# First chunk of a linear-attention and expert kernel: wide rows, one tile for all batches, work by head pairs, and a retuned planner

## The chip, the cores and the metric

The kernel runs on one core of a Trainium2 chip. The metric is device time in microseconds (us). "Before" and "after" are the two kernels of the change. Every run was timed beside runs of the kernel before on the same chip. Some executions are slower (for the kernel before 2.6 to 3.7 per cent longer); only fast runs are compared unless the text says otherwise.

Engine names in the profile: PE is TensorE (PEld its weight loads), DVE is VectorE, ACT is ScalarE, POOL is GpSimd, SP is SyncE. A "q" behind a name (SPq) is that engine's queue of instructions that issue transfers. L278 is line 278 of that kernel's source.

## The reference, cut to what matters

```
# q, k, v, f_logit: 4 batches x 8 heads x 768 tokens x 48
f = 1 / (1 + exp(-f_logit))
for t in range(768):                       # recurrent state of 48x48 per batch and head
    state = f[t][:, None] * state + outer(k[t], v[t])
    y[t]  = q[t] @ state
x = y as 3072 x 384                        # tokens x (heads * 48)
p = probs / (sum(probs) + 1e-9)            # 3072 x 4
out = sum over e of p[:, e] * (relu(x @ w1[e]) @ w2[e])   # 4 experts, 384 -> 1024 -> 384
```

## The kernel before

The 768 tokens are cut into six chunks of 128. In a chunk the recurrence becomes matmuls: prefix sums of the log gates (`cs`), exponentials of them (`e`), products with Q and K (`qk`), transposes, masked scores (`AT`), outputs (`y`), and an update of the state (`kv`). Chunk c+1's attention is woven into the expert matmuls of chunk c. In chunks 0 and 1 TensorE transposes Q and K; from chunk 2 on a DMA does it.

Nothing waits dynamically for a free engine. A planner in the kernel simulates all operations at build time, with assumed costs, and emits them in that order. The order is then fixed for each engine, while semaphores make each instruction wait until its data is there:

```
class Plan:
    LATENCY = 0.2                          # assumed delay between engines
    ...                                    # (cut) list scheduling by priority, costs, free buffers

def add_load(c, nm, b, n, prio, deps=()):  # a load takes 1.05 us per batch of the DMA's time, lands 2.0 later
    op = P.add(f"ld {nm}{c}.{b}", {"DMA": 1.05 * n}, lambda e: load(c, nm, b, n), prio,
               deps=deps, takes=[(nm, c, b // 2)], lag=2.0)
...
et = P.add(f"tp {c}.{b}", {"DMA": 1.8}, on(dma_tp), s(4), deps=[qm, km], ..., lag=2.2)   # DMA transposes
```

The first chunk is loaded batch by batch, 128 tokens on 128 partitions, in rows of 48 floats (192 bytes):

```
nc.sync.dma_start(out=tl(nm, c, b // 2)[:, hh(b, n), :], in_=srcs[nm][c, :, b * H:(b + n) * H, :])
for i, x in enumerate("f0 k0 q0 f1 k1 q1 f2 f3 k2 q2 v0 k3 q3 v1 v2 v3".split()):
    add_load(0, x[0], int(x[1]), 1, -1000 + i)
```

Of the kernel before, what the change touches and what calls it, by code (L numbers as in the profile page):

```python
# [14 lines left out]
class Op:  # L15


    def __init__(self, name, costs, emit, prio, deps=(), takes=(), frees=(), lag=0.0):
        self.name, self.costs, self.emit, self.prio = name, costs, emit, prio
        self.deps = [d for d in deps if d is not None]  # L20
        self.takes, self.frees, self.lag = list(takes), list(frees), lag
        self.end = self.start = self.engine = None
        self.pad = 0


class Plan:


    LATENCY = 0.2

    def __init__(self, rooms):
        self.ops, self.rooms = [], {r: list(range(n)) for r, n in rooms.items()}
        self.slot, self.left = {}, {}

# [14 lines left out]
    def take(self, o):  # L49
        new = [k for k in o.takes if k not in self.slot]  # L50
        for r in {k[0] for k in new}:
            if len(self.rooms[r]) < sum(k[0] == r for k in new):
                return False
        for k in new:
            self.slot[k] = self.rooms[k[0]].pop(0)
        return True

    def run(self):
# [5 lines left out]
        free_at.update({"DMA": 0.8, "DVE": 5.0, "POOL": 3.5, "ACT": 2.1, "PE": 2.0})  # L64
        freeing, done, now = [], [], 0.0
        while left:
# [3 lines left out]
            for e in ("PE", "ACT", "DVE", "POOL", "DMA"):  # L70
                while free_at[e] <= now + 1e-9:
                    for o in left:
                        if e in o.costs:
                            t = self.ready(o, e)
                            if t is not None and t <= now + 1e-9 and self.take(o):
                                break
                    else:
                        break
                    left.remove(o)
                    o.engine, o.start, o.end = e, now, now + o.costs[e]  # L80
                    free_at[e] = o.end
                    for k in o.frees:
                        self.left[k] -= 1
                        if self.left[k] == 0:
                            freeing.append((o.end + self.LATENCY, k[0], self.slot[k]))
# [14 lines left out]
def kernel(  # L100
# [23 lines left out]
    NT = B * T  # L124
    ctx.enter_context(tc.manual_schedule())
# [8 lines left out]
    rooms = {"ps_m": 4, "ps_t": 4, "f": 4, "q": 4, "k": 4, "v": 4, "ex": 2, "gp": 4, "e": 3, "qk": 7,  # L134
             "vb": 7, "egs": 8, "QK": 2, "AT": 2, "yb": 2, "xT": 2, "h": 2, "o": 6}
    P = Plan(rooms)

# [22 lines left out]
    )  # L160
    Sf = const.tile([MP, B, NP, D], FP32)
# [15 lines left out]
    for nm, a in (("f", f_logit), ("q", q), ("k", k), ("v", v)):  # L177
# [4 lines left out]
        "f": ([T, 2 * H, D], FP32), "q": ([T, 2 * H, D], FP32), "k": ([T, 2 * H, D], FP32), "v": ([T, 2 * H, D], FP32),  # L182
# [4 lines left out]
        "KV": ([T, 512], FP32), "xp": ([T, KD, T], BF16), "hp": ([128, NT], FP32), "op": ([128, 512], FP32),  # L187
    }

    def tl(kind, *key):  # L190

        if (kind, key) not in tiles:
            room = kind if kind in rooms else "ps_m" if kind in ("hp", "op") else "ps_t"
            slot = P.slot[(room, kind) + key if room.startswith("ps_") else (room,) + key]
            if room in ("gp", "qk"):
# [25 lines left out]
    def load(c, nm, b, n):  # L221
        ins[c, nm, b] = nc.sync.dma_start(out=tl(nm, c, b // 2)[:, hh(b, n), :],  # L222
                                          in_=srcs[nm][c, :, b * H:(b + n) * H, :])
        if (c, nm, b) == (1, "f", 0):
            after(ins[c, nm, b], ins["w", 5])

    def load_w(i, e, which):
        w, r = (w1_sb, w1_r) if which == 1 else (w2_sb, w2_r)
        ins["w", i] = nc.gpsimd.dma_start(out=w[:, e], in_=r[e])
        if i == 0:  # L230
            after(ins["w", 0], ins[0, "k", B - 1])

    p_src = moe_domain_probs.rearrange("(b c p) e -> p b c e", p=128, c=C)
    p_dst = pt.rearrange("p (b c) e -> p b c e", c=C)

    def load_p(c):
        nc.sync.dma_start(out=p_dst[:, :, c], in_=p_src[:, :, c])
# [8 lines left out]
    def gate1(c, b, n):  # L246
        nc.scalar.activation(out=tl("ex", c, b)[:, 0:n * H], in_=tl("f", c, b // 2)[:, hh(b, n), :], func=AF.Exp, scale=-1.0)  # L247
# [4 lines left out]

    def pe_cs(c, b):
        g, cs = tl("gp", c, b // 2)[:, b % 2], tl("cs", c, b)
        nc.tensor.matmul(out=cs[:, 0:HD], lhsT=Ub, rhs=g[:, :, 0:D], start=True, stop=True)  # L255
        if c == 0:
            for i in range(NP):
                nc.tensor.matmul(out=cs[0:MP, HD + i:HD + i + 1], lhsT=flat(g, i)[:, 0:MP], rhs=ones, start=True, stop=True)

    def exps(c, b):  # L260
        cs, e = tl("cs", c, b), tl("e", c, b)
        nc.scalar.activation(out=e[:, 0].rearrange("t (d h) -> t h d", d=D), in_=cs[:, 0:HD].rearrange("t (i r d) -> t r i d", r=2, d=D),  # L262
                             func=AF.Exp, scale=-1.0)
        nc.scalar.activation(out=e[:, 1], in_=cs[:, 0:HD], func=AF.Exp)  # L264
        if c == 0:
            nc.scalar.activation(out=tl("egs", c, b), in_=cs[0:MP, HD:HD + NP], func=AF.Exp, scale=-1.0)
# [6 lines left out]
    def product(c, b, j, eng):  # L273
# [3 lines left out]
                                   in0=tl("qk"[j], c, b // 2)[:, hh(b), :].rearrange("t (i r) d -> t i r d", r=2),  # L277
                                   in1=e, op=ALU.mult)  # L278

    def cast_v(c, b, eng):  # L280
        copy(eng, tl("vb", c, b), tl("v", c, b // 2)[:, hh(b), :])
# [21 lines left out]
    def ev_at(c, b, r):  # L303
        nc.vector.tensor_tensor(out=tl("AT", c, b)[:, r].rearrange("s i t -> s (i t)"),  # L304
                                in0=tl("A", c, b, r).rearrange("s i t -> s (i t)"), in1=mask01, op=ALU.mult)

    def pe_y(c, b):
        y, AT, vb, QK = tl("y", c, b), tl("AT", c, b), tl("vb", c, b), tl("QK", c, b)
        for i in range(NP):
            if c > 0:  # L310
                nc.tensor.matmul(out=y[:, i * 2 * D:(i + 1) * 2 * D], lhsT=QK[0:MP, 0, i, :],  # L311
                                 rhs=Sb[c % 2][:, b, i, :], start=True, stop=False, skip_group_check=True)
            for r in range(2):
                h = 2 * i + r
                nc.tensor.matmul(out=y[:, h * D:(h + 1) * D], lhsT=AT[:, r, i, :], rhs=vb[:, h, :],  # L315
                                 start=(c == 0), stop=True, skip_group_check=True)
# [13 lines left out]
    def state(c, b):  # L330
        egs, nb = tl("egs", c, b), Sb[(c + 1) % 2]
# [37 lines left out]
    def store(c, nt, cols):  # L369
        r0 = nt * S + c * T  # L370
        nc.sync.dma_start(out=out[r0:r0 + T, cols], in_=tl("o", c, nt)[:, cols])
# [5 lines left out]
    def add_load(c, nm, b, n, prio, deps=()):  # L377
        op = P.add(f"ld {nm}{c}.{b}", {"DMA": 1.05 * n}, lambda e: load(c, nm, b, n), prio,
                   deps=deps, takes=[(nm, c, b // 2)], lag=2.0)
# [4 lines left out]
    for i, x in enumerate("f0 k0 q0 f1 k1 q1 f2 f3 k2 q2 v0 k3 q3 v1 v2 v3".split()):  # L384
        add_load(0, x[0], int(x[1]), 1, -1000 + i)
    wd = {}
    for i, (e, which) in enumerate(nw):
        iss = P.add(f"w issue {i}", {"POOL": 0.9}, lambda _, i=i, e=e, which=which: load_w(i, e, which),
                    -500 + i, deps=[ld[0, "k", B - 1]])
        wd[e, which] = wd[i] = P.add(f"w {i}", {"DMA": 4.5}, lambda _: None, -500 + (0, 1, 2, 3, 4, 5, 101.5, 103.5)[i], deps=[iss], lag=2.0)  # L390
    for half in range(2):
        for j, nm in enumerate("fkqv"):
            add_load(1, nm, 2 * half, 2, -400 + 4 * half + j, deps=[wd[5]])


    xdone, kvdone = {}, {}

    def attention(c, slot, gran):
        G, X, Y, GS = {}, [], [], []
        more = c < C - 1  # L400
        for b0 in range(0, B, gran):
            p, d, half = slot(b0, 0) - 0.5, 0.54 if gran == 1 else 0.84, b0 // 2
            g1 = P.add(f"gate1 {c}.{b0}", {"ACT": d}, lambda e, b0=b0: gate1(c, b0, gran), p,
                       deps=[ld[c, "f", b0]], takes=[("ex", c, b0)], frees=[("f", c, half)])
# [4 lines left out]
        for b in range(B):  # L409
# [5 lines left out]
            cs = P.add(f"cs {c}.{b}", {"PE": 0.17 if c else 0.36}, on(pe_cs), s(0),  # L415
                       deps=[G[b]], takes=[pt_("cs")], lag=0.2, frees=[("gp", c, half)])
            ex = P.add(f"exps {c}.{b}", {"ACT": 0.98 if c else 1.1}, on(exps), s(0) + 0.1, deps=[cs],
                       takes=[("e", c, b)] + ([("egs", c, b)] if c == 0 else []), frees=[pt_("cs")])
            GS.append(P.add(f"egs {c}.{b}", {"DMA": 1.0}, on(dma_egs), s(3), deps=[ex], takes=[("egs", c, b)],
                            frees=[("e", c, b)], lag=2.0) if c and more else None)  # L420
            pe = {"DVE": 0.6, "POOL": 1.0} if c < 2 else {"POOL": 1.0}
            qm = P.add(f"q {c}.{b}", pe, one(product, 0), s(4) - 0.2,
                       deps=[ex, ld[c, "q", b]], takes=[("qk", c, b)], frees=[("q", c, half), ("e", c, b)])
            km = P.add(f"k {c}.{b}", pe, one(product, 1), s(4) - 0.1,
                       deps=[ex, ld[c, "k", b]], takes=[("qk", c, b)], frees=[("k", c, half), ("e", c, b)])
            vb = P.add(f"v {c}.{b}", {"ACT": 0.52, "DVE": 0.36} if c == 0 else {"POOL": 0.5, "ACT": 0.52} if c == 1 else {"POOL": 0.5}, one(cast_v), s(4),
                       deps=[ld[c, "v", b]], takes=[("vb", c, b)], frees=[("v", c, half)])
            if c < 2:
                tq = P.add(f"tpq {c}.{b}", {"PE": 0.22}, on(pe_tp, 0), s(4), deps=[qm],
                           takes=[pt_("tp")], frees=[("qk", c, b)], lag=0.2)  # L430
                tk = P.add(f"tpk {c}.{b}", {"PE": 0.22}, on(pe_tp, 1), s(4) + 0.01, deps=[km],
                           takes=[pt_("tp")], frees=[("qk", c, b)], lag=0.2)
                et = P.add(f"ev_tp {c}.{b}", {"DVE": 0.69, "ACT": 1.05}, lambda e, b=b: copy(e, tl("QK", c, b)[0:MP], tl("tp", c, b)), s(4) + 0.1,
                           deps=[tq, tk], takes=[("QK", c, b)], frees=[pt_("tp")])
            else:
                et = P.add(f"tp {c}.{b}", {"DMA": 1.8}, on(dma_tp), s(4), deps=[qm, km], takes=[("QK", c, b)],
                           frees=[("qk", c, b)], lag=2.2)
            at = P.add(f"at {c}.{b}", {"PE": 0.35}, on(pe_at), s(7), deps=[et],
                       takes=[pt_("A", 0), pt_("A", 1)], lag=0.2, frees=[("QK", c, b)])
            eA = [P.add(f"ev_at{r} {c}.{b}", {"DVE": 0.7}, on(ev_at, r), s(7) + 0.1 + 0.1 * r, deps=[at],  # L440
                        takes=[("AT", c, b)], frees=[pt_("A", r)]) for r in range(2)]
            y = P.add(f"y {c}.{b}", {"PE": 0.4 if c else 0.28}, on(pe_y), s(11), deps=eA + [vb, kvdone.get((c - 1, b))],
                      takes=[pt_("y")], frees=[("QK", c, b), ("AT", c, b), ("vb", c, b)], lag=0.2)
# [4 lines left out]
            if c < 2:  # L448
                xt = P.add(f"xt {c}.{b}", {"PE": 0.17}, on(pe_xt), s(13), deps=[ey],
                           takes=[pt_("xp")], frees=[("yb", c, b)], lag=0.2)  # L450
# [3 lines left out]
            else:  # L454
                xdone[c, b] = P.add(f"xt {c}.{b}", {"DMA": 0.9}, on(dma_xt), s(13), deps=[ey], takes=[("xT", c)],
                                    frees=[("yb", c, b)], lag=2.2)
            X.append(xdone[c, b])
        for b in range(B if more else 0):
            on = lambda f, b=b: (lambda e: f(c, b))
            pt_ = lambda kind, b=b: ("ps_t", kind, c, b)  # L460
            s15 = slot(b, 15) if c else 2 + 2 * b
            kv = P.add(f"kv {c}.{b}", {"PE": 0.22}, on(pe_kv), s15, deps=[Y[b], X[B - 1] if c == 0 else None],
                       takes=[pt_("KV")], frees=[("vb", c, b), ("qk", c, b)], lag=0.2)
# [127 lines left out]
```

## Time and profile before

| | before |
|---|---|
| time | 305.1 us, median of the four runs (304.5 to 315.0, the last slow) |
| span of the profiled execution | 302.7 us, mean granted TensorE clock 0.999 |
| first expert matmul | 22.7 us |
| TensorE gaps over 0.3 us after 45 us | 1.0 us in all |

The second is the busy time in the stretch from 70 to 125 us, in which chunk 2's attention begins (columns: stretch, its length, then busy us and instructions of PE, PEld, DVE, ACT, POOL, granted clock, DMA share, GB/s):

```profile
70.00:125.00 55.00, 54.24 (x454) 34.76 (x460) 33.32 (x71) 33.08 (x62) 29.29 (x51) 1.00 0.85 163
```

### The profile page before, as it was taken

Reading aid. Unit: us, or ns where it says so; the run is one execution under the profiler, and the core shown is the slowest. Engines: PE = TensorE matmul, PEld = TensorE weight load, DVE = VectorE, ACT = ScalarE, POOL = GpSimd, SP = SyncE. Lnnn points to the kernel's source line nnn. Section 1 sums busy time; section 2 is a strip of 40 time slices with the busy share of each in tenths; the row PEclk is TensorE's granted clock in tenths of the full one; section 3 lists DMA queues with packets and bytes.
Section 4 is the critical chain, followed back from the end, with each engine's and each line's share of the span. In section 5 each row is a group of like instructions: output and inputs, shape, how many; then the busy total and the mean of one; then the engine's idle time right before and its main releaser. Section 6 shows DMA issues by size and latency. Waiting matters only on the chain.

```text
span 302.7 us, 5517 instructions
## 1 busy us (share of the span) xinstructions
PE 293.2 (97%) x2112; PEld 169.4 (56%) x2143; DVE 138.1 (46%) x273; ACT 170.8 (56%) x295; POOL 95.5 (32%) x157
## 2 busy tenths in 40 slices
PE   7899999999999999999999999999999999999995
PEld 5565555567775655455555555555555555555553
DVE  6774013787853764516555344544423443201223
ACT  5767654857865444676356475345566344475440
POOL 4584400409656237423426143522332100000000
PEclk9999999999999999999999999999999999999999
DMA  7999999954994589866997877301322201100003
GB/s 157 203 193 204 207 206 193 228 83 91 217 207 84 111 161 187 189 122 120 182 187 134 216 142 147 56 13 28 100 61 51 48 14 30 67 22 2 0 0 106
DMA packets 137355, 36.10 MB, mean 119 GB/s; under 512 B 128496, under 2 KB 135792, under 8 KB 137328
## 3 DMA queue, kind: packets, MB, share of 16 engines
q1 hardware_dynamic: 131568, 29.45, 49.1%
q0 software_dynamic: 5760, 6.29, 12.4%
q8 instruction: 17, 0.28, 0.4%
q14 instruction: 10, 0.08, 0.1%
HBM read 31.51 MB, written 4.72 MB: 120 GB/s over the span
## 4 chain that ended last, share of the span: by engine, by line
PE 88%; DMA 4%; DVE 2%; SPq 2%; issue 1%; POOL 1%; ACT 1%; DVEq 0%; ACTq 0%; POOLq 0%
PE ps_m L356 41%; PE ps_m L344 40%; DMA w_sb<-in_moe_w_dram 3%; PE ps_t L300 2%; SPq L222 2%; DMA f<-in_f_logit_dram 1%; PE ps_t L315 1%; PE ps_t L321 1%; PE ps_t L311 1%; PE ps_t L255 1%; PE ps_t L285 1%; DVE qk L276 1%; POOL qk L276 0%; DVE AT L304 0%; POOL Sf L335 0%
## 5 line engine op out<-in xcount | busy, mean ns | idle before, releaser
L352 ACT ACTIVATE h<-ps_m 128x512 bf16<-128x512 f32 (+1 forms) x171 | 98.3, 577 | 103.0 <-PE ps_m L344 92.9
L356 PE MATMUL ps_m<-w_sb,h 128*128 128x384 bf16 x776 | 153.0, 324 | 0.2
L344 PE MATMUL ps_m<-xT,w_sb 128*128 128x512 bf16 (+1 forms) x593 | 150.4, 362 | 2.1 <-DVE o L367 0.3
L356 PEld LDWEIGHTS <-h 128*128 128x128 bf16 x776 | 73.0, 98 | 57.0
L363 DVE SCALAR_TENSOR_TENSOR o<-ps_m,pn,o 128x384 f32<-128x384 f32 (+1 forms) x73 | 44.6, 611 | 96.8 <-PE ps_m L356 89.4
L344 PEld LDWEIGHTS <-w_sb 128*128 128x128 bf16 x624 | 59.8, 98 | 47.1 <-issue 0.7
L276 POOL TENSOR_TENSOR qk<-q,e 128x384 bf16<-128x384 f32 x19 | 22.8, 1204 | 64.9 <-ACT e L262 64.4
L304 DVE TENSOR_TENSOR AT<-ps_t,mask 128x512 bf16<-128x512 f32 x48 | 31.1, 683 | 19.2 <-PE ps_t L300 19.1
L335 POOL TENSOR_TENSOR Sf<-Sf,egs 48x192 f32<-48x192 f32 x40 | 20.4, 510 | 48.8 <-DVE Sf L328 46.8
L350 DVE TENSOR_SCALAR h<-ps_m 128x512 bf16<-128x512 f32 (+1 forms) x37 | 20.7, 572 | 22.0 <-PE ps_m L344 19.8
L276 POOL TENSOR_TENSOR qk<-k,e 128x384 bf16<-128x384 f32 x20 | 21.0, 1052 | 19.8 <-ACT e L264 12.9
L262 ACT ACTIVATE e<-ps_t 128x384 f32<-128x384 f32 x24 | 20.7, 864 | 3.7 <-PE ps_t L255 2.4
L328 DVE TENSOR_TENSOR Sf<-Sf,ps_t 48x192 f32<-48x192 f32 x40 | 14.0, 349 | 6.1 <-PE ps_t L321 5.3
L336 POOL CAST sb<-Sf 48x192 bf16<-48x192 f32 x40 | 13.6, 339 | 2.6
L365 ACT ACTIVATE o<-ps_m,pn 128x384 f32<-128x384 f32 x20 | 11.6, 580 | 3.9 <-PE ps_m L356 3.1
L264 ACT ACTIVATE e<-ps_t 128x384 f32<-128x384 f32 x24 | 13.0, 541 | 0.0
L556 PE MATMUL ps_m<-busy 128*128 128x256 bf16 x71 | 11.5, 301 | 1.3 <-DVE busy L140 1.3
L218 DVE CAST yb<-ps_t 128x384 bf16<-128x384 f32 x16 | 8.9, 555 | 7.4 <-PE ps_t L315 6.3
L247 ACT ACTIVATE ex<-f 128x768 f32<-128x768 f32 (+1 forms) x14 | 10.5, 748 | 3.1 <-DMA f<-in_f_logit_dram 2.9
L315 PE MATMUL ps_t<-vb,AT 128*128 128x48 bf16 x192 | 11.4, 184 | 0.7 <-DVE vb L218 0.7
L315 PEld LDWEIGHTS <-AT 128*128 128x128 bf16 x192 | 9.8, 97 | 3.0 <-issue 1.0
L251 ACT ACTIVATE gp<-ex 128x768 bf16<-128x768 f32 (+1 forms) x14 | 10.5, 751 | 0.4
(50 smaller groups left out, 139.9 us busy)
## 6 DMA issues: line engine op xcount, KB each, us to landing
w_sb<-in_moe_w_dram POOLq DMA_DIRECT2D x8, 768.0 KB, 18.8
out_dram<-o SPq DMA_DIRECT2D x23, 192.0 KB, 2.1
f<-in_f_logit_dram SPq DMA_DIRECT2D x10, 384.0 KB, 4.3
k<-in_k_dram SPq DMA_DIRECT2D x10, 384.0 KB, 5.2
q<-in_q_dram SPq DMA_DIRECT2D x10, 384.0 KB, 5.3
v<-in_v_dram SPq DMA_DIRECT2D x10, 384.0 KB, 5.5
f<-in_f_logit_dram SPq DMA_DIRECT2D x4, 192.0 KB, 4.0
k<-in_k_dram SPq DMA_DIRECT2D x4, 192.0 KB, 4.0
```

Of the source, the lines that this page charges most:

```text
L262: nc.scalar.activation(out=e[:, 0].rearrange("t (d h) -> t h d", d=D), in_=cs[:, 0:HD].rearrange("t (i r d) -> t r i d", r=2, d=D), func=A ...
L276: engines[eng].tensor_tensor(out=tl("qk", c, b)[:, j, :, 0:D].rearrange("t (i r) d -> t i r d", r=2), in0=tl("qk"[j], c, b // 2)[:, hh(b), ...
L304: nc.vector.tensor_tensor(out=tl("AT", c, b)[:, r].rearrange("s i t -> s (i t)"), in0=tl("A", c, b, r).rearrange("s i t -> s (i t)"), in1= ...
L315: nc.tensor.matmul(out=y[:, h * D:(h + 1) * D], lhsT=AT[:, r, i, :], rhs=vb[:, h, :], start=(c == 0), stop=True, skip_group_check=True)
L328: nc.vector.tensor_tensor(out=Sf[rows, b], in0=Sf[rows, b], in1=KV[rows, :, r, :], op=ALU.add)
L335: nc.gpsimd.tensor_tensor(out=Sf[rows, b], in0=Sf[rows, b], in1=eg, op=ALU.mult)
L336: nc.gpsimd.tensor_copy(out=nb[rows, b, :, r * D:(r + 1) * D], in_=Sf[rows, b])
L344: nc.tensor.matmul(out=tl("hp", c, e, fc, n0)[:, n0:n1], lhsT=w1_sb[:, e, kk, fc * 128:(fc + 1) * 128], rhs=tl("xT", c)[:, kk, n0:n1], sta ...
L350: nc.vector.tensor_relu(out=dst, in_=src)
L352: nc.scalar.activation(out=dst, in_=src, func=AF.Relu)
L356: nc.tensor.matmul(out=tl("op", c, e, nt, part)[:, cols], lhsT=tl("h", c, e)[:, fc, nt * T:(nt + 1) * T], rhs=w2_sb[:, e, fc, cols], start ...
L363: nc.vector.scalar_tensor_tensor(out=o, in0=op, scalar=pe, in1=o, op0=ALU.mult, op1=ALU.add)
```

## The change

The intent was a shorter first chunk. Gates, K and Q come in rows of 768 bytes: a partition holds four tokens in a row of one batch, so that one tile of 128 partitions holds 32 groups of four tokens times four batches. The attention of chunk 0 then works on pairs of heads for all batches at once. V can't follow, because its rows have to match the scores; it is loaded in a permuted token order. K has to be brought back to one batch per tile for the state update, by 16 transfers inside SBUF. Chunk 0's stores are cut in four. And the planner is retuned. Cut to the core:

```diff
-    LATENCY = 0.2
+    LATENCY, AHEAD = 0.07, 0.06
...
+                    if o.ring is not None:
+                        self.ring = max(self.ring, o.end) + o.ring
+                        o.end = max(o.end, self.ring - 4.0)      # the queue may run 4 us ahead of the data
+                        o.lag = self.ring - o.end + 1.6
...
-    rooms = {..., "f": 4, "q": 4, "k": 4, "v": 4, ...
+    rooms = {..., "f": 2, "q": 2, "k": 2, "v": 2, ...             # whole-chunk tiles
...
+        if nm == "v":
+            src = v.rearrange("b h (c p j) d -> c j p (b h) d", p=R, j=J)[0, x]
+            d = nc.sync.dma_start(out=tl("v", 0)[x * R:(x + 1) * R], in_=src)        # 32 neighbouring partitions
+        else:
+            src = a.rearrange("b h (c p j) d -> c b p h (j d)", p=R, j=J)[0, x]
+            eng = nc.scalar if nm in "fk" and x % 2 else nc.sync
+            d = eng.dma_start(out=tl(nm, 0)[x::B].rearrange("p (h j) d -> p h (j d)", j=J), in_=src)
...
+    def dma_k0(b):
+        for j in range(J):
+            nc.sync.dma_start(out=tl("qk", 0, b)[j * R:(j + 1) * R, 1], in_=tl("k0")[b::B, j])
...
-        op = P.add(f"ld {nm}{c}.{b}", {"DMA": 1.05 * n}, ..., lag=2.0)
+        op = P.add(f"ld {nm}{c}.{b}", {"DMA": 0.6}, ..., ring=1.0 * n)
...
-                et = P.add(f"tp {c}.{b}", {"DMA": 1.8}, ..., lag=2.2)
+                et = P.add(f"tp {c}.{b}", {"DMA": 1.25}, ..., ring=0.5)
... # (cut) attention0 by head pairs; lag of TensorE work 0.2 -> 0.05; other transfers; weight issue order
```

## The prediction

> **What bounds the kernel now.** I read the profile in this order: busy shares, the chain of waits, then the first 33 us in order of time. The busy shares first (engine, busy us, share of the span, instructions):
>
> ```profile
> PE 293.2 (97%) x2112; PEld 169.4 (56%) x2143; DVE 138.1 (46%) x273; ACT 170.8 (56%) x295; POOL 95.5 (32%) x157
> ```
>
> TensorE is the bound, but its share also counts dummy matmuls on the tile `busy`, which run while the first chunk is prepared. The span has two parts. From 22.74 us on (first matmul of the experts) TensorE is dense: in the trace's single records a 512-column matmul starts every 0.216 us, a 384-column one every 0.163, and beyond gaps of one missing record I find only two stalls after 23 us, 0.46 at 69.6 and 0.51 at 80.9. Before 22.74 nothing useful for the end is done except the first chunk. The change reworks just that part, so it can move the end only by moving the start of the dense part, or by tearing holes into it. The chain of waits, cut to the first 24 us (start, length, what):
>
> ```profile
> 5.39 1.24 SPq L222
> ...
> 6.67 4.10 DMA f<-in_f_logit_dram
> ...
> 10.79 0.53 ACT ex L247
> ...
> 13.03 1.36 POOL qk L276
> 14.38 0.25 issue
> 14.63 8.07 DMA w_sb<-in_moe_w_dram
> 22.70 0.05 issue
> 22.74 0.39 PE ps_m L344
> ```
>
> The start is set by the first weight load W0. GpSimd issues it at 14.63, after its third K product and after the last K load; it takes 8.07 us. The other arm, the attention of chunk 0, ends almost together: its last eviction into xT starts at 21.96 and takes 0.48. Both arms must shrink for a gain. The order of time at the start of the dense part (start, length, engine, line):
>
> ```profile
> 21.96 0.48 ACT L216 COPY xT<-ps_t 128x384 bf16<-128x384 bf16 x1 [0.73 <-PE ps_t L340]
> ...
> 28.72 3.40 PE L344 MATMUL ps_m<-xT,w_sb 128*128 128x512 bf16 x14
> 31.96 1.30 PE L356 MATMUL ps_m<-w_sb,h 128*128 128x384 bf16 x7
> ```
>
> TensorE does 13 first-layer units (three matmuls each) before its first second-layer matmul at 31.96, which needs the third weight load, W2. Those 13 units are what covers W2. The stretches and the DMA issues of the start (columns of a stretch: busy us of PE, PEld, DVE, ACT, POOL with counts, clock, DMA share, GB/s; of an issue: KB, us to landing):
>
> ```profile
> 4.00:6.00 2.00, 1.57 (x13) 1.12 (x12) 1.06 (x2) 1.24 (x3) 0.00 (x0) 1.00 1.06 207
> ...
> pt<-in_moe_domain_probs_dram SPq DMA_DIRECT2D x1, 8.0 KB, 10.5
> ```
>
> The DMA engines are full at 207 GB/s while ACT, DVE and GpSimd are largely idle: early on the loads limit.
>
> [...] a 192-byte packet takes 15 ns of its engine, a 768-byte one (only in the last stores) 36 ns, so four times the bytes in 2.4 times the time. [...] the probabilities, 512 packets of 16 bytes beside the weights, ran at about 100 packets per us against 100 of the 2048-byte weight packets, and took 10.5 us to land. [...] Here a GpSimd K product took 1.34 to 1.36 us when it overlapped a VectorE product, 1.00 beside VectorE work that reads PSUM.
>
> **The change part by part.**
> *Loads.* Twelve loads (gates, K, Q) go from 64 packets per DMA engine to 16: 16 x 36 ns = 0.58 us instead of 64 x 15 ns = 0.96. V keeps 192 bytes. First data was at 1.91, so V3 is in at 1.91 + 12 x 0.58 + 4 x 0.96 = 12.7, against 18.63 before (there slowed by W0); landing adds 0.7 to 1.0 (gates: data end 2.99, use 3.72; W0: 21.73, 22.70), so 13.5. But every gate now needs four loads; half are issued by ACT, perhaps behind its 1.28 us table load. I take 5.6 for all gates, against 3.72 for the first batch.
> *ACT.* Two Exp at 0.84, four Ln at 0.52, four pairs with two plain Exp of 0.54 and a small one of 0.16: 8.7 us. The permuted Exp of 0.86 becomes plain. The instruction order has one eviction (0.6) inside, so the last pair's gates are ready near 5.6 + 8.7 + 0.6 = 14.9, and 15.0 with gaps.
> *TensorE.* The prefix sums grow from 384 to 1536 columns per unit, about 0.5 us each, in time otherwise filled with dummies. After the first expert matmul the two programs have the same work: I counted the same number of matmuls of each size.
> *GpSimd* is the new narrow place. Its order is: Q product of pair 0, W0, three casts of V, Q of pair 2, Q of pair 3, K of pair 3, then W1 to W7. W0 goes out near 11 (Q lands near 9.7, product 1.3) and lands near 19, no longer the bound. The casts wait for all four V loads: 13.5. Three casts at steps of 0.45 (the uncontended 0.50 overlaps a little), 0.3 for one held up by a VectorE product, three products at 0.95 each: 13.5 + 1.4 + 0.3 + 2.9 = 18.1.
> *From there to the first expert matmul:* transposes 0.48, eviction 0.6, scores 0.45, two masks 1.4, output 0.4, eviction 0.6, transposes 0.4, eviction 0.6 = 4.9. The first two of a unit's three matmuls don't need this last piece (0.43), so the dense part begins as if at 18.1 + 4.5 = 22.6. Before: 22.74. The attention arm gains 0.1.
> *W2.* W1 now leaves GpSimd only at 18.1. From issue to first packet W0 took 2.2 (14.63 to 16.83); W1 and W2 took 8.9 together (21.57 to 30.51); landing 0.95. So W2 lands at 18.1 + 2.2 + 8.9 + 0.95 = 30.2. The new program also sends 16 transfers of K (512 packets of 1 KB), to bring K back to one batch per tile, at just that time. From 36 ns at 768 bytes and 65 at 1536 I estimate 45 ns: 32 packets per engine make 1.4 us of engine time, of which I count 1.2 as delay: 31.4. In the instruction order the first second-layer matmul stands after nine units, not 13: 27 x 0.216 + 16 small matmuls x 0.052 = 6.7 us after the start, at 29.3. (The same count with 13 units gives 22.74 + 8.4 + 0.8 = 31.97 for the kernel before; observed 31.96.) TensorE would wait 31.4 - 29.3 = 2.1 us.
> *Sum:* -0.1 + 2.1 = +2.0, that is 306.9; without the delay by the K transfers +0.8, 305.7. The retuned order of the later chunks might remove the two stalls (-1.0) or, with its smaller allowances for latency, add some. I place the value between, at 305.9.
> *Beside other work, costing nothing:* chunk 0's stores in four pieces, the split probabilities, and the sums' extra columns.
>
> **The rivals.**
> First, a clean gain: the attention arm is as short as ACT allows. After 14.9, ACT still has four evictions of 0.6, three of 0.5 and three of 0.55, so xT could be full at 20.9, and with the overlap of 0.43 the dense part starts near 20.5: 302.7. For it: loads are the first wait in the chain of before, and they get 4.6 us shorter. Against: GpSimd has about 4.6 us of casts and products after the last V load, and W1 waits behind them; V is not helped by wider rows.
> Second, a larger loss. If the GpSimd products meet VectorE's products and take 1.35, 18.1 becomes 19.2, and the start and W2 move with it: 308. The K transfers could also be starved as the probabilities were (10.5 us) and hold up the small matmuls that update the state. Against: these stand before the W2 wait, so most of such a delay hides behind it.
> Third, a wash: the prefetch order suits, W2 is in time, and both arms end as before: 304.8.
> Fourth, holes in chunk 1: its loads still wait for the sixth weight load, which I expect within 1 us of the 42.2 of before, and its attention is squeezed from 25 to 20 us of TensorE's work. That could cost 1 to 2. For it: both stalls of the kernel before are in this chunk.
>
> **Range and chances.** The two large uncertainties are the GpSimd chain (1 us either way, and it counts fully) and the W2 wait (0 to 3). Together with the stalls of chunk 1 they give 303.0 to 308.6 for eight in ten. Two per cent is 6.1 us. To win that, the dense part would have to start at 16.6, only 1.6 us after ACT has the last gates by my sums: 0.02. To lose it needs a wait of over 6 us in the weights or in chunk 1: 0.04. The rest, 0.94, is within 2%.
>
> **What would show it right or wrong.** Right: 768-byte packets near 36 ns; the last V landing at 13 to 14; GpSimd's last K product ending near 18 and the W1 issue directly after it; first expert matmul between 22 and 23; a gap of 1 to 3 us before the first second-layer matmul, ended by the DMA of the weights, near 31. Wrong, upward in speed: K product by 16.5, or the second layer starting below 29.4 (31.96 less four units of 0.65) without a gap. Wrong, downward: the V rows slower than 15 ns per packet[...], or stalls of several us in the small matmuls of chunk 1.

## More of the kernel before

The runs were made in several batches on different chips. The fast runs of the kernel before have medians of 304.9 to 305.5 in the batches of the experiments, so I compare times across batches, to about 1 us.

TensorE's waits from 45 to 175 us (who waited, for whom: total us, how often, longest):

```profile
PE ps_m L344 <- DVE o L367: 0.3, 1, 0.3
PE ps_t L285 <- DVE qk L276: 0.3, 1, 0.3
```

TensorE never waits for a DMA transpose.

## The result, and the profile after

The kernel after took 333.5 us (median of 4, 332.7 to 338.2, the last slow) against 305.1 before. The ratio is 1.093, with a 95% interval of 1.090 to 1.096: 28.4 us slower. A ratio here and below is the mean time of one kernel's fast runs over that of the other's in the same rounds, so it is not quite the ratio of the medians. The profiled run of after has a span of 330.9 us and a mean granted clock of 0.979.

The busy shares and the granted clock of the kernel after, from its page (the clock in tenths, 40 slices of the span):

```profile
PE 301.3 (91%) x2111; PEld 173.4 (52%) x2142; DVE 137.5 (42%) x272; ACT 168.7 (51%) x294; POOL 103.6 (31%) x169
PEclk9979999999999699997999999999999999999999
```

TensorE's share fell from 97 to 91 per cent at the same amount of expert work. There is no new busy engine; TensorE waits. The granted clock was 0.50 in three short stretches (3.4 us from 20.7, 6.8 from 106.0 and 3.4 from 153.8), each beside a gap in TensorE's work (it was busy for 0.48 us of 18 to 20, 1.49 of 103 to 106 and 0.57 of 150 to 154). The chain of waits of the first 40 us (start, length, what):

```profile
11.50 5.00 DMA v<-in_v_dram
...
16.66 2.11 POOL vb L261 x3
18.77 1.92 POOL qk L345 x2
20.69 0.97 POOL h L345
...
26.48 5.65 DMA qk<-h
...
32.14 5.99 DMA qk<-h
...
38.17 0.41 PE ps_t L451 x4
```

V lands at 16.5, GpSimd casts it and makes its three products in 5.0 us, and then the K transfers (`qk<-h`) take over the chain until 38.1. In the order of time, the masks of the last two pairs, and the first expert matmuls, which the records start at 28.5:

```profile
24.03 2.48 DVE L435 TENSOR_TENSOR AT<-ps_t,mask 128x512 bf16<-128x512 f32 x4 [1.47 <-PE ps_m L370]
...
28.48 1.46 PE L474 MATMUL ps_m<-xT,w_sb 128*128 128x512 bf16 x5
```

So the first expert matmul is 5.8 us later than before. Measured at the last state matmuls (`kv`) of chunk 0, which in both programs stand behind eight expert units, the lateness is 38.2 against 28.5 us: 9.7. The rest is lost later. The same stretch as shown of before, and TensorE's wait for the DMA transposes from 45 to 175 us:

```profile
70.00:125.00 55.00, 44.87 (x441) 30.62 (x444) 34.58 (x70) 29.47 (x54) 26.95 (x43) 0.94 0.78 131
```

```profile
PE ps_t L431 <- DMA QK<-qk: 11.6, 5, 3.4
```

TensorE is busy for 44.9 instead of 54.2 us of the stretch from 70 to 125 us. My sum of TensorE's gaps over 0.3 us after 45 us is 17.0 us against 1.0 in all before. Together 9.7 + 16.0 = 25.7 of the 28.2 by which the spans differ. The remaining 2.5 fits the halved clock and waits under 0.3 us: in the two stretches at half clock after 45 us, the matmuls without a gap over 0.3 us lost 3.4 us against their normal spacing.

### The profile page after: what moved, and what is told of

Same layout as the page of the kernel before. It is cut to its first block, busy times and chain, and to the rows that moved or that the text cites. A ratio compares the mean times of both kernels' runs of the same rounds, so it can differ in the third digit from the quotient of the medians.

```text
span 330.9 us, 5574 instructions
## 1 busy us (share of the span) xinstructions
PE 301.3 (91%) x2111; PEld 173.4 (52%) x2142; DVE 137.5 (42%) x272; ACT 168.7 (51%) x294; POOL 103.6 (31%) x169
## 4 chain that ended last, share of the span: by engine, by line
PE 70%; DMA 15%; SPq 6%; POOL 4%; issue 3%; ACT 1%; DVE 0%; DVEq 0%; POOLq 0%
PE ps_m L486 33%; PE ps_m L474 31%; DMA QK<-qk 5%; DMA qk<-h 4%; DMA v<-in_v_dram 3%; SPq L265 3%; DMA k<-in_k_dram 2%; PE ps_t L431 2%; POOL vb L261 1%; SPq L385 1%; POOL qk L407 1%; DMA out_dram<-o 1%; PE ps_t L445 1%; PE ps_t L441 1%; PE ps_t L451 1%
## 5 line engine op out<-in xcount | busy, mean ns | idle before, releaser
L486 PE MATMUL ps_m<-w_sb,h 128*128 128x384 bf16 x776 | 156.0, 326 | 0.3
L474 PE MATMUL ps_m<-xT,w_sb 128*128 128x512 bf16 (+1 forms) x593 | 153.8, 364 | 2.4 <-DVE o L493 0.5
L435 DVE TENSOR_TENSOR AT<-ps_t,mask 128x512 bf16<-128x512 f32 x48 | 31.1, 685 | 28.6 <-PE ps_t L431 25.0
L261 POOL CAST vb<-v 128x384 bf16<-128x384 f32 x21 | 11.9, 584 | 40.9 <-DMA v<-in_v_dram 19.4
L407 POOL TENSOR_TENSOR qk<-k,e 128x384 bf16<-128x384 f32 x18 | 17.9, 997 | 6.4 <-ACT e L397 6.3
L431 PE MATMUL ps_t<-QK 48*128 48x128 bf16 x160 | 8.2, 227 | 12.5 <-DMA QK<-qk 11.6
L394 ACT ACTIVATE e<-ps_t 128x384 f32<-128x384 f32 x20 | 17.3, 865 | 4.0 <-PE ps_t L389 3.0
L431 PEld LDWEIGHTS <-QK 48*128 48x128 bf16 x160 | 4.7, 98 | 19.6 <-DMA QK<-qk 13.8
L497 DVE TENSOR_SCALAR o<-ps_m,pn 128x384 f32<-128x384 f32 x6 | 3.7, 618 | 21.2 <-PE ps_m L486 21.2
L306 ACT ACTIVATE ex<-f 128x768 f32<-128x768 f32 x10 | 8.4, 841 | 4.8 <-DMA f<-in_f_logit_dram 4.8
L451 PEld LDWEIGHTS <-qk 128*112 128x112 bf16 x80 | 7.1, 135 | 7.1 <-DMA qk<-h 3.4
```

The costliest lines, as they stand in the source:

```text
L261: engines[eng].tensor_copy(out=out, in_=in_)
L394: nc.scalar.activation(out=e[:, 0].rearrange("t (d h) -> t h d", d=D), in_=cs[:, 0:HD].rearrange("t (i r d) -> t r i d", r=2, d=D), func=A ...
L407: engines[eng].tensor_tensor(out=tl("qk", c, b)[:, j, :, 0:D].rearrange("t (i r) d -> t i r d", r=2), in0=tl("qk"[j], c)[:, b * H:(b + 1) ...
L431: nc.tensor.matmul(out=tl("A", c, b, r)[:, i, :], lhsT=QK[rows, 1, i, :], rhs=QK[rows, 0, i, :], start=True, stop=True)
L435: nc.vector.tensor_tensor(out=tl("AT", c, b)[:, r].rearrange("s i t -> s (i t)"), in0=tl("A", c, b, r).rearrange("s i t -> s (i t)"), in1= ...
L474: nc.tensor.matmul(out=tl("hp", c, e, fc, n0)[:, n0:n1], lhsT=w1_sb[:, e, kk, fc * 128:(fc + 1) * 128], rhs=tl("xT", c)[:, kk, n0:n1], sta ...
```

## The experiments

My first theory (A) was that the new first chunk is late, for causes in its transfers, and that this lateness alone makes the later holes, because the order of transfers on SyncE is fixed. The rival (B) was that the retuned plan makes the later holes itself. All kernels are edits of one of the two.

Summary of what follows (gaps: as defined above, after 45 us; first: first expert matmul in the profiled run); six further runs stand in the text alone:

| run | what | first | gaps | time | ratio |
|---|---|---|---|---|---|
| before | | 22.7 | 1.0 | 305.1 | |
| after | | 28.5 | 17.0 | 333.5 | 1.093 |
| p1_plan_only | new plan, old first chunk | 25.6 | 13.5 | 320.0 | 1.049 |
| t1_old_load_cost | p1, old cost of loads | 25.4 | 5.5 | 311.0 | 1.020 |
| t2_old_other_costs | p1, other old costs of transfers | 24.8 | 11.8 | 318.2 | 1.043 |
| q3_old_transfer_costs | p1, all old costs of transfers | 25.4 | 4.3 | 311.0 | 1.019 |
| q4_new_chunk_old_plan | new first chunk, old plan constants | 29.7 | 4.0 | 319.9 | 1.047 |
| q5_new_chunk_new_latency | after, old costs of transfers only | 28.3 | 6.7 | 320.6 | 1.050 |
| r2_k_by_tensore | q4, K returned by TensorE | 32.0 | 5.8 | 317.5 | 1.040 |
| r4_k_tensore_v_rows | r2, V over 128 partitions (wrong result) | 28.6 | 4.4 | 312.4 | 1.025 |

### The plan alone

```diff
 # after.py, with chunk 0 loaded and worked on as in the kernel before
-    for i, x in enumerate("f0 f1 f2 f3 k0 k1 ...
+    for i, x in enumerate("f0 k0 q0 f1 k1 q1 f2 f3 k2 q2 v0 k3 q3 v1 v2 v3".split()):
-    attention0(lambda b, s: -200 + 1.6 * b + s * 0.8)
+    attention(0, lambda b, s: -200 + 3.6 * b + s * 0.8, 1)
```

> The first chunk is loaded and worked on as in the kernel before; the rest of the change stays (whole-chunk tiles, smaller latencies in the planner, its new costs for transfers, loads of chunk 1 and later as the new plan orders them). Theory A (the new first chunk is late by some 10 us, and the later holes come from an order of transfers that was fixed for an early first chunk): first expert matmul at 22.5 to 23.5, chunk-2 loads on time, time 302 to 308. Rival B (the retuned plan or the whole-chunk tiles tear the later holes by themselves): the holes between 70 and 170 us stay, time 316 to 324.

Measured: 320.0 us (319.5 to 321.2), ratio 1.049 (1.046 to 1.052). My theory A fell: without the new first chunk, 14.9 of the 28.4 us are there. TensorE's waits of this run from 45 to 175 us begin with the same wait as in after:

```profile
PE ps_t L328 <- DMA QK<-qk: 7.9, 6, 3.1
```

### The order of SyncE's queue

```diff
 # after.py: two stores of chunk 0 behind the loads of chunk 2 in the emitted order
+    for late, early in (("store 0.0.0", "ld v2.0"), ("store 0.1.0", "ld k2.2")):
+        done.remove(at[late])
+        done.insert(done.index(at[early]) + 1, at[late])
```

> The changed kernel with one edit in the order of SyncE's queue: the stores of chunk 0's first two tiles go behind the chunk-2 loads instead of ahead of them, as in the kernel before. Theory A (SyncE stands at these stores, which wait for a TensorE that is 10 us late, and the chunk-2 loads stand behind them): chunk-2 loads start near 73 instead of 79.66, the gaps between 79 and 120 us (about 11 us with the half clock) fall to under 4, time 322 to 328. Rival B (holes from the retuned plan itself): the holes stay within 2 us, time 331 to 335.

Measured: 334.2 us, ratio 1.095 (1.092 to 1.097). No gain. Its profiled run was a slow one, so I read only the order from it: the first chunk-2 load did not come near 73, because the queue now stood at the small state transfers of chunk 1, which wait for ScalarE:

```profile
70.78 9.37 SPq L402 DMA_DIRECT2D egs<-e  x6
80.19 0.59 SPq L265 DMA_DIRECT2D f<-in_f_logit_dram  x1
```

Moving one wait in the queue only put another in its place. The theory of these two stores fell.

### Buffers, latencies, costs of transfers

The new plan has three parts that could do it: whole-chunk tiles, smaller latencies, and new costs of transfers. One run each.

```diff
 # q1: before.py with whole-chunk tiles, nothing else
-    "f": 4, "q": 4, "k": 4, "v": 4,
+    "f": 2, "q": 2, "k": 2, "v": 2,
 # q2: plan-only kernel with the old latencies
-    LATENCY, AHEAD = 0.07, 0.06        (and lag=0.05 -> lag=0.2)
+    LATENCY, AHEAD = 0.2, 1e-9
 # q3: plan-only kernel with the old costs of transfers
-        {"DMA": 0.6} ... ring=1.0 * n   (and so for transposes, stores, probabilities, state transfers)
+        {"DMA": 1.05 * n} ... lag=2.0
```

> The kernel before with only its buffers changed: gates, K, Q, V in two whole-chunk tiles instead of four half-chunk tiles, and the loads of a chunk planned after the last load of the chunk before it. Old planner. Theory C (the 13.5 us of holes in the plan-only run come from the planner's constants): no effect, 304 to 306.5. Rival D (a whole-chunk tile comes free only when all four batches are done with it, so loads start late and VectorE, GpSimd and TensorE wait for them): 309 to 318.

> The plan-only kernel with the old latencies back (0.2 between engines and 0.2 behind TensorE work instead of 0.07 and 0.05; no starting 0.06 early); the new costs of transfers and the whole-chunk tiles stay. If the small latencies tear the holes: holes beyond 45 us fall from 13.5 to under 4, time 306 to 311. If the costs of transfers do: holes of 9 to 14 stay, time 316 to 322.

> The plan-only kernel with the old costs of transfers back (a load costs its full 1.05 us per batch of queue time and lands 2.0 later; transposes 1.8 and 2.2 later; no ring that lets the queue run 4 us ahead); the small latencies stay. If the transfer model tears the holes: time 306 to 311. If the small latencies do: holes of 9 to 14 us stay, time 316 to 322.

q1: three of its four runs fell in the slow state, and so did its profile. The one fast run took 305.8 us, inside the range of before's fast runs beside it (304.8 to 306.0). I take the tiles as harmless on this one run. Its slow profile doesn't speak against it: the gaps after 45 us are 1.0 there, as in before, and the loss is at the start, where the first expert matmul comes at 34.3.

q2: 329.0 us, ratio 1.073, outside both expectations. Its total doesn't decide, because something else happened at its start: its chain of waits holds one V load that took 15.06 us to land, so its first expert matmul came only at 36.8. The slow profile of q1 has the same event (start, length, what; q2, then q1):

```profile
14.37 15.06 DMA v<-in_v_dram
```

```profile
14.67 15.24 DMA v<-in_v_dram
```

So q2's runs near 329 may well be slow ones. Less the 11.2 us by which it starts later than the plan-only run, 329.0 would be about 318, which is an estimate and fits the second expectation. Its gaps after 45 us can be read too: 10.1 of 13.5 stay. The latencies are not the main cause.

q3: 311.0 us, ratio 1.019 (1.015 to 1.023). The old costs of transfers take away 9.0 of the plan's 14.9 us.

### Which cost

```diff
 # t1: plan-only kernel, only the loads' cost as before
-        {"DMA": 0.6}, ... takes=[(nm, c)], ring=1.0 * n)
+        {"DMA": 1.05 * n}, ... takes=[(nm, c)], lag=2.0)
 # t2: plan-only kernel, only the other transfers' costs as before (transposes 1.8 and 2.2, ...)
```

> The plan-only kernel (320.0) with the old cost of loads alone back (2.1 us of queue time for a load of two batches, landing 2.0 later); the new costs of transposes, stores and the small state transfers stay. If the cost of loads is what tears the holes (the plan lets the queue run 4 us ahead of the data and so puts chunk 2's attention at 93.5 us where the old plan had 99.4): 309 to 313, like all old costs together (311.0). If the other costs do: 317 to 321.

> The plan-only kernel with the old costs of transposes, stores, probabilities and small state transfers back; the new cost of loads stays. If the cost of loads is the cause: holes as in the plan-only run, 317 to 322. If the others are: 309 to 313.

t1: 311.0 us (310.6 to 311.4), as good as all old costs together. t2: 318.2 us, 1.8 less than the plan-only run, which is little more than the noise. It is the cost of the loads. What it changes is best seen in two views. The issue of the first two transposes of chunk 2 in the plan-only run, and then in t1 (start, length, queue, transfer):

```profile
92.85 1.34 SPq L317 DMA_TRANSPOSE QK<-qk  x1
...
96.17 1.26 SPq L317 DMA_TRANSPOSE QK<-qk  x1
```

```profile
93.25 1.33 SPq L317 DMA_TRANSPOSE QK<-qk  x1
...
96.58 1.25 SPq L317 DMA_TRANSPOSE QK<-qk  x1
```

The transposes are issued at the same time in both, even 0.4 us later in the faster kernel. But TensorE's wait for them in t1 is this, against the 7.9 above:

```profile
PE ps_t L328 <- DMA QK<-qk: 1.0, 1, 1.0
```

What moved is TensorE's own order. Counted in the emitted instructions, the scores of chunk 2's first batch stand behind 102 expert units (62 of the first layer and 40 of the second) in the plan-only kernel, behind 112 in t1, 115 in the kernel before and 100 in after. A unit is about 0.65 us, so the new plan puts these scores 6.5 us earlier in TensorE's program than t1 does, on the promise that the loads cost the queue 0.6 us each and may run 4 us ahead. The chip's queue doesn't keep it: in the plan-only run the eight loads of chunk 2 hold the queue from 76.6 to 90.2, 1.7 us each. The first and the last of them:

```profile
76.57 0.58 SPq L248 DMA_DIRECT2D f<-in_f_logit_dram  x1
...
88.47 1.71 SPq L248 DMA_DIRECT2D v<-in_v_dram  x1
```

TensorE reaches the scores too early and stands, since its order is fixed.

### The new first chunk alone

```diff
 # q4: after.py with LATENCY 0.2, lags 0.2 and the old costs of transfers;  q5: after.py with the old costs only
```

> The changed kernel with both old latencies and old costs of transfers: the new first chunk alone, under the old planner. Theory: what is left is the first chunk's own lateness, 5.4 us of later start (28.14 against 22.74) plus up to 3.9 us of waits for the K transfers, and few holes after 45 us (under 4): 312 to 319. Rival (the new first chunk itself pushes SyncE's queue so far back that chunk 2 and 3 fall into holes under any plan): 324 to 334.

> The changed kernel with only the old costs of transfers back (small latencies stay). The old costs were worth 9 us in the plan-only pair (320.0 to 311.0). If the transfer model is what tears the later holes in the changed kernel too: 321 to 326. If the small latencies matter more here: 328 to 333.

q4: 319.9 us, ratio 1.047, just above the expected range; q5: 320.6, ratio 1.050, just below its first range. The gaps after 45 us are 4.0 and 6.7 instead of 17.0. TensorE's wait for the transposes from 45 to 175 us in q5, against the 11.6 of after:

```profile
PE ps_t L431 <- DMA QK<-qk: 2.7, 3, 1.4
```

So in the changed kernel too the costs of transfers make most of the later holes (333.5 - 320.6 = 12.9 us); the latencies' 0.7 is within the noise. The first chunk under the old constants costs 319.9 - 305.6 = 14.3 us, the plan alone 14.9; together 29.2, against 28.4 for the change as a whole. The two losses nearly add, but not term by term: the costs of transfers are worth 12.9 us here and 9.0 in the plan-only pair. Also, q4 keeps those parts of the new plan that are not these constants (whole-chunk tiles, weights as a queue of their own, split exponentials), and so does the plan-only run; what they cost is counted in both.

### K's way back

```diff
 # k4: after.py with 4 transfers over 128 partitions (takes the wrong tokens: wrong result on purpose)
-        for j in range(J):
-            nc.sync.dma_start(out=tl("qk", 0, b)[j * R:(j + 1) * R, 1], in_=tl("k0")[b::B, j])
+        nc.sync.dma_start(out=tl("qk", 0, b)[:, 1], in_=tl("k0")[:, b])
 # r2: q4 without any K transfer; TensorE transposes the transposed K once more, 4 evictions (right result)
+            nc.tensor.transpose(out=tl("kb", 0, i)[:, b, 0:MP], in_=<K of pair i, batch b>, identity=ident[0:MP, 0:MP])
 # wl: q4 with weight loads W3 to W7 issued behind the first state update
+    for x in issues[3:]:
+        x.deps.append(kvdone[0, 0])
```

> K brought back by 4 transfers over 128 partitions instead of 16 over 32; same bytes, same packets of 1 KB; the result is wrong on purpose (K of the wrong tokens). Theory A (16 issues of about 0.65 us and landing behind the weights make the K transfers late): issue falls from 10.97 to about 3 us, last K lands at 30 to 32 instead of 38.1, the three TensorE gaps before the small state matmuls (3.9 us together) go, time 327 to 331. Rival (the packets share the engines with the weights, however they are issued): last landing still beyond 36, time within 1 us of 333.5.

> The new first chunk under the old planner (319.9), with the 16 K transfers replaced by 16 TensorE transposes of the already transposed K and 4 evictions; right result. Theory A (the K transfers cost the waits before the state matmuls and hold up SyncE's queue): the gaps before these matmuls (3.5 us) go; some 4 evictions of about 0.5 join the first chunk, of which up to 1.5 may delay the start; time 315.5 to 318. Rival (the waits just move on to the weights of the second layer, which land at 34): time 318.5 to 321.

> The new first chunk under the old planner with its K transfers, but the weight loads W3 to W7 issued by GpSimd only behind the first state update; W1 and W2 stay. Theory E (transfers that SyncE issues while GpSimd issues weight loads start about 4 us late): the first K packet follows its issue within 2 us instead of 4.3, the last K transfer lands 2 to 4 us earlier than at 38.7, gaps before the state matmuls under 1.5 us; time 316 to 320, since W3 is late in exchange. Rival (K packets wait for their own issues, one per 0.68 us, and share the engines with the weights): the first packet still over 3.5 us after its issue.

k4: 331.2 us, ratio 1.085; 2.3 us less than after. The issue of the K transfers in after and in k4, each from its order of time:

```profile
21.68 10.97 SPq L385 DMA_DIRECT2D qk<-h  x16
```

```profile
21.29 3.03 SPq L384 DMA_DIRECT2D qk<-h  x4
```

A transfer of 32 partitions cost the queue 0.69 us and one of 128 partitions, with four times the bytes, 0.76: here the price was per transfer. The same 512 packets of 1 KB ran at about 50 per us in after, which is 32 per issue of 0.69 us, and at up to 131 in k4. The three gaps before the state matmuls (0.9, 1.1 and 1.8 us) were gone, and the last state matmuls were 4.0 us earlier. But some 1.7 of that was lost again later, where the gaps were 18.7 instead of 17.0.

r2: 317.5 us, 2.4 less than q4, as expected, though its first chunk became 2.3 us longer (32.0 against 29.7) through the added transposes and evictions.

wl: 319.6 us, no change. The theory that GpSimd's issue of weights holds the transfers back fell: with that issue ending at 24.9, the chain of waits still has a K transfer issued at 24.5 that landed 5.87 us later,

```profile
24.49 5.87 DMA qk<-h
```

and all packets but the first transfer's 32 began only after 28. In after, k4, q4 and wl alike the bulk of the packets starts 5.0 to 5.4 us behind the first issue. Why is left open; what can be said is that the next weight load fills the engines in this time (about 100 packets of 2 KB per us).

### V's rows

```diff
 # n2: after.py with natural token order in chunk 0: V and stores whole; the eviction of the transposes permutes
+            d = nc.sync.dma_start(out=tl("v", 0)[:, x * H:(x + 1) * H, :], in_=srcs["v"][0, :, x * H:(x + 1) * H, :])
+        copy(eng, tl("QK", 0, i)[0:MP, x].rearrange("m b (p j) -> m j p b", j=J),
+             tl("tp", 0, i)[:, x].rearrange("m j (p b) -> m j p b", b=B))
 # r4: r2 with V in plain order (wrong result on purpose)
+            d = nc.sync.dma_start(out=tl("v", 0)[:, x * H:(x + 1) * H, :], in_=srcs["v"][0, :, x * H:(x + 1) * H, :])
```

> Natural token order inside chunk 0: V as four loads over 128 partitions, one load of the probabilities per chunk, chunk-0 stores whole (4 transfers instead of 16); the eviction of the transposes permutes instead. Q, K, gates and the 16 K transfers stay. Theory A (V is late because each load fills only 32 neighbouring partitions): V casts start at 14 to 15 instead of 16.66, first expert matmul 1.5 to 2.5 earlier than 28.2, and 12 fewer store issues take about 7 us out of SyncE's queue, time 320 to 328. Rival (V waits for its place in SyncE's queue and for bandwidth, not for partitions): casts still at 16 or later, time 329 to 334.

> The same, and V loaded in plain token order by four loads over all 128 partitions (the result is wrong on purpose: V's rows don't fit K's). Theory A (V in 32 partitions per load arrives 3 us late, as the V casts at 13.58 in the token-order run showed against 16.66, and GpSimd's casts, products and W1 stand behind it): V casts start near 13.7, first expert matmul 2 to 3.5 us earlier than in the run beside it, time 312 to 315. Rival (ScalarE's chain of gates sets the start anyway): gain under 1 us.

n2: 340.0 us, ratio 1.113, slower than anything. The K transfers write every fourth partition in this version. The V part worked; the casts began at 13.58 instead of 16.66:

```profile
13.58 1.40 POOL L261 CAST vb<-v 128x384 bf16<-128x384 f32 x3
```

But my permuting eviction cost 2.56 us each instead of 0.59. Groups by shape on ScalarE from 12 to 36 us, first of n2, then of after (line, operation, count, busy us, mean ns of one):

```profile
L259 ACT COPY QK<-ps_t 112x512 bf16<-112x512 bf16 x5 | 11.8, 2561 | 10.8 <-PE ps_t L348 10.8
```

```profile
L259 ACT COPY QK<-ps_t 112x512 bf16<-112x512 bf16 x5 | 2.8, 587 | 6.4 <-PE ps_t L353 6.4
```

Neighbouring elements were written 256 bytes apart. That pushed the first expert matmul to 42.3.

r4: 312.4 us, ratio 1.025; 5.1 less than r2 and at the good end of the range. Its first expert matmul came at 28.6 instead of 32.0. In the single records V's four loads took 5.9 to 6.9 us from first to last packet in the profiled runs of all seven kernels that load V into 32 neighbouring partitions (6.0 in after, 6.9 in r2), and 5.0 and 4.9 in n2 and r4. The last V data was in at 15.7 in after, 16.9 in r2, 14.6 in n2 and 14.5 in r4. Slower packets are only a part of it: a 192-byte packet took 25 ns (median) in after, but 15 in r2, as in n2, r4 and the kernel before; the mean of r2 is 22 against 17 in r4. The rest of the cause is open. Besides, a load over 128 partitions serves a whole batch, so the first cast needs one load and not four.

Still, r4 is 7 us behind the kernel before. Its last K product ends at 19.5, near my predicted 18.1, but the first expert matmul comes 9.1 us after it. Part of that is VectorE's masks of the last two pairs, again four in a row:

```profile
23.89 2.48 DVE L438 TENSOR_TENSOR AT<-ps_t,mask 128x512 bf16<-128x512 f32 x4 [0.58 <-PE ps_t L363]
```

No version that I tried beats the kernel before.

## Why the prediction was wrong, point by point

- **"36 ns for a 768-byte packet", "W1 directly after the K product", the GpSimd chain.** Right. The packets took 36 ns (median; 40 on average), W1 was issued at 21.60 right after the product, and casts and products took 5.0 us where I had 4.6. One reading was too wide: the K products of 1.34 to 1.36 us began after the VectorE product that they overlapped; at 68.36 of before one that began first took 1.00.
- **"V3 is in at 1.91 + 12 x 0.58 + 4 x 0.96 = 12.7 ... so 13.5."** Failed: 15.7 and 16.5. The twelve wide loads were nearly right (V's first packet at 9.70 where my sum has 8.87; the first data of all came at 2.33 instead of 1.91). V was mis-sized: 9.70 to 15.69 is 6.0 us instead of 3.84. In after its packets took 25 ns and not 15; that they might be slower I had named among the things that would make me wrong. Loads into 32 neighbouring partitions took 5.9 us or more in every version, also where the median packet took 15. Landing took the 0.8 that I had.
- **"I take 5.6 for all gates."** They were there at 6.85. It cost nothing: ScalarE had the last pair's exponentials at 17.0, and GpSimd made the last K product only from 20.69 on.
- **"From there to the first expert matmul ... 4.9", taken as 4.5.** Failed, a size: it was 28.5 - 21.65 = 6.85 us. I had two masks (1.4 us) in it; four ran one behind the other (2.48), because the pair before the last was late too. The two errors explain the start: 22.6 + (21.65 - 18.1) + (6.85 - 4.5) = 28.5.
- **The W2 wait of 2.1 us, and "most of such a delay hides behind it".** Failed. The K transfers themselves were the wait. I counted engine time for their packets (1.2 us) and not 16 issues of 0.69 us and the 5 us before most of the packets start. The second rival of my text had the mechanism and dismissed it. The K transfers came to 3.9 us of gaps; removing them was worth 2.3 us (k4) and 2.4 (r2).
- **"The retuned order of the later chunks might remove the two stalls (-1.0) or ... add some."** This step failed most: the plan alone costs 14.9 us. I treated a change of assumed costs as a detail of order. Shown: the loads' cost makes 9.0 of it, by placing chunk 2's scores 6.5 us too early in TensorE's program (t1 against the plan-only run: 7.9 to 1.0 us of waits). The remaining 5.9 us of the plan I did not split: t1 still starts 2.7 us later than before and has 4.5 us more gaps.
- **The fourth rival, "its loads still wait for the sixth weight load ... could cost 1 to 2".** It looked at the wrong chunk. In after the gaps between 45 and 75 us are 0.3; between 75 and 125 they are 11.2.
- **Chances.** I gave a loss of over 2 per cent 0.04, on the ground that it needs a wait of over 6 us in the weights or chunk 1. The range was built from the first chunk's terms only; the term that I had not worked out, the retuned plan, was worth 14.9 us alone.

## What to carry to other kernels

In a program whose order is fixed at build time, the assumed cost of a transfer decides where its consumer stands in an engine's stream. Here the optimistic cost was paid as a stall of TensorE (7.9 us of waits), and the old, higher one left 1.0, since other work filled the place. When a change retunes a planner, compare the positions of the consumers with the measured times of the producers, before anything else. Count transfers as well as bytes: here 16 transfers of 32 partitions held the issuing queue for 10.97 us, and 4 of 128 partitions with the same bytes for 3.03.
